# First weight-sum units loaded behind the eighth attention step, summed from the twelfth, and gate columns loaded one step later

## The chip, the cores and the metric

One core of a Trainium2 chip runs the whole program. The metric is the device time of one launch in microseconds (us). Engines: PE does matmuls, DVE elementwise work, ACT activations, POOL small things and the issue of "software" DMAs (queue q0), SP the issue of most other DMAs (queue q1). Times inside a trace are us from the first instruction; the device time is 1.8 us longer than that span. In the lines of a trace, `arena` is the one large on-chip buffer in which the program places most of its tensors, so it stands for many of them.

## The reference

An adaptive-layer-norm transformer block on one prompt of 2048 rows:

```python
h = layernorm(x) * (1 + ca) + sa
q = (h @ wq) -> 32 heads;  k, v: the last 512 cached rows of 4 kv heads
x = x + ga * (softmax(q k^T / sqrt(128)) v) @ wo
h = layernorm(x) * (1 + cb) + sb
x = x + gb * ((silu(h @ w_gate) * (h @ w_up)) @ w_down)
# sa, ca, ga, sb, cb, gb = silu(c) @ w_mod, each 1024 wide
```

## The kernel before

Large products are done as seven smaller ones (Strassen's scheme), for which sums of weight blocks are needed. Each attention runs in 64 numbered steps (0 to 63, then 64 to 127). During the first attention DVE makes those of wo in 16 "units" of 512 KB: POOL loads a unit, DVE makes four sums in two ticks, POOL stores it to DRAM. The second attention does the same for w_down in 14 units.

Every instruction goes through a small tracker. It makes the issuing engine wait for the last writer of what it reads, and for the last writer and *all readers* of what it writes:

```python
def op(self, st, emit, reads=(), writes=()):
    for b in reads:   # wait for b.last_write
    for b in writes:  # wait for b.last_write and for every entry of b.reads
    ...
    for b in reads:   b.reads[st] = c
    for b in writes:  b.last_write = (st, c); b.reads = {}
```

The helpers that the change touches, and the steps of attention that they lie between (cuts marked with `...`):

```python
def unit_load(end):
    ...
    T.op(Q_of[slot][0], lambda: g.dma_start(dst, src), writes=[w.b_raw, w.b_s3])   # g is POOL

def unit_chain(k0, k1):
    unit_load(k1)
    unit_load(k1)
    yield
    for k in range(k0, k1):      # two ticks a unit: two sums; two sums, store, next load
        ...

def pv(i):
    ...                          # 16 matmuls into PSUM banks 5 and 6
    r = i % 2
    T.op(DVE, reciprocal(rl[r] <- PSUM), writes=both + [B_rl[r]])
    T.op(DVE, o_s <- PSUM * rl[r], reads=[B_rl[r]], writes=both + [...])
    ...                          # transposing DMA of o_s

def pre0(i):                     # start of step i of the first attention
    if i in (7, 8):
        load_wga(i - 7)          # 1 MB of gate columns each, needed in steps 12 to 14
    ...
    if i in (8, 9):              # second half of the rows: modulate the transposed norm
        for dt in range(4 * (i - 8), 4 * (i - 8) + 4):
            modulate(hT[1], B_hT[1], dt, ...)
    ...                          # query projection; norm_turn issues the transposes of nsc into hT[1]

# step i: pre0(i); scores(i-1); pv(i-2); tick0(i)
def tick0(i):
    ...
    if i == 8:
        chain[0] = unit_chain(0, HP)
    if 8 <= i < NI - 8:
        unit_tick(i)             # skips i % 4 == 3 and 21..24
```

The softmax here doesn't subtract the row's maximum and nothing guards it: scores larger than these inputs give would overflow.

## Time and profile before

| | before |
|---|---|
| device time, median of the first 3 runs | 1164.04 us (1162.75 to 1164.68) |
| device time of the profiled run, span | 1161.61, 1159.8 us |
| PE busy | 1143.1 us, with 86 of 7105 matmul records missing from this trace |
| wait of the modulation for the transpose | 2.10 us |
| PE idle behind it | 1.97 us |

The missing records are why PE's busy times of different traces are not compared below. What can be compared is the distance between two landmarks: the reciprocal of step 7 and that of step 12. The loads are issued before the first of the two, but every wait of DVE and PE that the change removes or makes in the first attention lies between them. Timeline columns: start, duration, engine, line, operation, and in brackets the idle time just before and what ended it.

```profile
49.99 0.18 DVE L824 RECIPROCAL rl<-ps 128x4 f32<-128x4 f32 x1 [1.19 <-PE ps L272]
...
71.03 0.18 DVE L824 RECIPROCAL rl<-ps 128x4 f32<-128x4 f32 x1 [1.68 <-PE ps L272]
```

The stretch is 71.03 - 49.99 = 21.04 us.

### The profile page before, as it was taken

What the parts mean: (1) busy time and instruction counts of PE and PEld (TensorE: products, weight loads), DVE (VectorE), ACT (ScalarE), POOL (GpSimd) and SP (SyncE); (2) the same over time, 40 slices, a digit from 0 to 9 for tenths busy, and PEclk for the clock granted to TensorE, in tenths of its full rate; (3) what the DMA queues carried; (4) which work ended last, traced back from release to release, by engine and by line L of the source; (5) the groups of instructions that cost most, each with busy time, mean ns of one, the idle gap of its engine ahead of it and who ended that gap; (6) DMA issues with size and microseconds to landing.
All of it is one profiled execution on the core that took longest, in us unless ns stands there. A gap on an engine that the chain in (4) does not pass through costs nothing.

```text
span 1159.8 us, 18164 instructions
## 1 busy us (share of the span) xinstructions
PE 1143.1 (99%) x7019; PEld 588.2 (51%) x7105; DVE 817.5 (70%) x1638; ACT 532.5 (46%) x745; POOL 68.8 (6%) x137
## 2 busy tenths in 40 slices
PE   8899999999999999999999999999999999999999
PEld 5565556654446666556444444444444444444444
DVE  4758997657576777776567898767558777776536
ACT  3866777730117777787110344454110444544110
POOL 1200221000000111111000010000000000000000
PEclk9999999999999999999999999999999999999999
DMA  9878899966906898844865232333764424234443
GB/s 326 178 188 202 217 214 219 204 169 188 261 10 170 190 205 195 212 94 108 202 192 172 78 104 73 102 81 100 209 197 143 123 74 109 73 93 131 131 162 110
DMA packets 289941, 179.98 MB, mean 155 GB/s; under 512 B 130496, under 2 KB 278080, under 8 KB 289856
## 3 DMA queue, kind: packets, MB, share of 16 engines
q1 hardware_dynamic: 226880, 92.31, 35.8%
q10 hardware_dynamic: 54336, 55.05, 14.9%
q0 software_dynamic: 8640, 31.46, 9.1%
q8 instruction: 56, 0.92, 0.3%
q14 instruction: 29, 0.24, 0.1%
HBM read 128.45 MB, written 19.92 MB: 128 GB/s over the span
## 4 chain that ended last, share of the span: by engine, by line
PE 94%; DVE 2%; DMA 1%; ACT 1%; issue 1%; SPq 0%; POOL 0%; DVEq 0%; ACTq 0%
PE ps L272 94%; ACT arena L805 1%; DMA arena<-nsc 1%; DVE arena L835 1%; DMA arena<-in_w_mod_dram 0%; DVE arena L906 0%; PE ps L276 0%; DVE st L413 0%; SPq L310 0%; DVE arena L432 0%; SPq L341 0%; DVE arena L852 0%; ACT tmp L743 0%; DVE arena L1563 0%; ACT L1548 0%
## 5 line engine op out<-in xcount | busy, mean ns | idle before, releaser
L272 PE MATMUL ps<-arena 128*128 128x512 f16 (+2 forms) x6714 | 1135.4, 329 | 13.8 <-POOL arena L406 2.2
L272 PEld LDWEIGHTS ps<-arena 128*128 128x128 bf16 (+1 forms) x6800 | 578.0, 98 | 564.8 <-DVE arena L835 6.3
L805 ACT ACTIVATE arena<-ps 128x1024 bf16<-128x1024 f32 x256 | 261.3, 1021 | 45.9 <-PE ps L272 33.9
L838 ACT ACTIVATE tmp<-ps 128x512 f32<-128x512 f32 x167 | 99.7, 597 | 297.8 <-PE ps L272 283.7
L906 DVE TENSOR_TENSOR arena<-arena 128x512 f16<-128x512 bf16 x328 | 133.5, 420 | 3.0
L835 DVE TENSOR_TENSOR arena<-ps,tmp 128x512 bf16<-128x512 f32 (+1 forms) x134 | 91.9, 686 | 49.3 <-PE ps L272 37.8
L838 ACT ACTIVATE nsc<-ps 128x512 f32<-128x512 f32 x84 | 50.1, 596 | 93.2 <-PE ps L272 90.9
L827 DVE TENSOR_TENSOR arena<-ps,rl 128x512 f16<-128x512 f32 x128 | 88.5, 691 | 4.9 <-DVE rl L824 0.5
L835 DVE TENSOR_TENSOR arena<-ps,nsc 128x512 f16<-128x512 f32 x84 | 57.4, 687 | 41.2 <-PE ps L272 29.9
L824 DVE RECIPROCAL rl<-ps 128x4 f32<-128x4 f32 x128 | 23.1, 180 | 88.0 <-PE ps L272 87.0
L1548 ACT ACTIVATE arena<-arena 128x512 f16<-128x512 f16 x84 | 49.9, 624 | 32.4 <-DVE arena L835 32.4
L1044 DVE TENSOR_TENSOR arena<-arena 128x2048 f16<-128x2048 f16 (+3 forms) x56 | 56.2, 1013 | 9.3 <-PE ps L272 8.8
L1120 DVE TENSOR_TENSOR tmp<-ps,tmp 128x512 f32<-128x512 f32 x32 | 22.1, 690 | 57.0 <-ACT tmp L838 47.3
L838 ACT ACTIVATE arena<-ps 128x512 f32<-128x512 f32 x16 | 9.6, 597 | 89.0 <-PE ps L272 89.0
L956 DVE TENSOR_TENSOR arena<-arena 128x512 f16<-128x512 bf16 x120 | 48.0, 421 | 1.9 <-DMA arena<-in_A_wo_dram 0.8
L413 DVE BATCH_NORM_STATS2 st<-x_res 128x6 f32<-128x512 bf16 x58 | 39.6, 683 | 3.9 <-DMA x_res<-in_A_x_dram 3.7
L1563 DVE TENSOR_TENSOR arena<-arena 128x512 f16<-128x512 f16 x84 | 35.1, 418 | 0.3
L1121 DVE TENSOR_TENSOR tmp<-tmp,rowb 128x512 f32<-128x512 f32 (+1 forms) x49 | 33.6, 686 | 1.7
L427 DVE TENSOR_SCALAR nsc<-x_res,mv,rstd 128x1024 f16<-128x1024 bf16 (+1 forms) x30 | 16.2, 541 | 24.1 <-DMA arena<-nsc 23.4
L603 DVE SCALAR_TENSOR_TENSOR arena<-arena 128x1024 bf16<-128x1024 bf16 x24 | 29.2, 1217 | 0.0
L1122 DVE TENSOR_TENSOR arena<-tmp,x_res 128x512 bf16<-128x512 f32 (+1 forms) x33 | 22.3, 675 | 1.1
L835 DVE TENSOR_TENSOR arena<-ps,rowb 128x512 f16<-128x512 f32 x28 | 19.3, 690 | 3.9 <-ACT rowb L838 3.4
(87 smaller groups left out, 333.9 us busy)
## 6 DMA issues: line engine op xcount, KB each, us to landing
arena<-in_A_wq_dram SPq DMA_DIRECT2D x28, 512.0 KB, 5.2
arena<-wo_sum ACTq DMA_DIRECT2D x7, 2048.0 KB, 8.7
arena<-in_B_w_gate_dram SPq DMA_DIRECT2D x28, 512.0 KB, 4.1
arena<-in_B_w_up_dram SPq DMA_DIRECT2D x28, 512.0 KB, 4.9
arena<-wd_sum ACTq DMA_DIRECT2D x8, 1792.0 KB, 7.8
arena<-in_B_w_down_dram ACTq DMA_DIRECT2D x6, 1792.0 KB, 7.2
arena<-in_A_wo_dram POOLq DMA_DIRECT2D x16, 512.0 KB, 4.9
wo_sum<-arena POOLq DMA_DIRECT2D x16, 512.0 KB, 4.7
```

Source lines behind the costliest of these rows:

```text
L272: T.op(PE, lambda: TE.matmul(out_ap, lhsT, rhs, start=start, stop=stop, skip_group_check=skip), reads=reads, writes=[bank_buf])
L413: T.op(DVE, lambda: V.bn_stats(st_[sl][:, hf * 6:hf * 6 + 6], x_res[:, t, hf * 512:hf * 512 + 512]), reads=[B_x[t]], writes=[B_st[sl]])
L805: T.op(ACT, lambda: A.activation(ex_s[es][:, 2 * kp:2 * kp + 2, :], banks2(SCB + 2 * kp), AF.Exp, scale=att_scale), writes=[PB[SCB + 2 * k ...
L827: T.op(DVE, lambda: V.tensor_tensor(o_s[os_].rearrange("p (a b) d -> p a b d", a=2), psap(PVB * 512, [[512, 2], [130, 2], [1, P]]), rlb, A ...
L835: T.op(DVE, lambda: V.tensor_tensor(out, bank(ba), other, ADD), reads=[ob2], writes=[PB[ba], ob])
L838: T.op(ACT, lambda: A.activation(dst, bank(bk), AF.Copy), writes=[PB[bk], db])
L906: T.op(st, lambda: eng.tensor_tensor(o, a, b, op), reads=rd, writes=[wr])
L956: T.op(DVE, lambda: V.tensor_tensor(o, a, b, SUB), reads=rd, writes=[wr])
L1044: T.op(DVE, lambda: V.tensor_tensor(o, a, b, SUB), reads=rd, writes=[sb])
L1121: T.op(DVE, lambda: V.tensor_tensor(tm, tm, rw, MULT), reads=[B_row[row]], writes=[tb])
L1548: T.op(ACT, lambda: A.activation(o, s_, AF.Silu), reads=[sb], writes=[ob])
L1563: T.op(DVE, lambda: V.tensor_tensor(gu[blk][:, p, :], o, s_, MULT), reads=[sb, ob], writes=[B_gu[blk][p]])
```

## The change

The intent: the two first unit loads, free to start long before their step, crowd the transposing DMAs of the next norm. They are to start later; so are the gate columns; and the sums begin when the data are surely there. To hold the loads back they are declared to read rl, which the attention steps write.

```diff
-            def unit_load(end):
+            def unit_load(end, ahead=()):
...
-                T.op(Q_of[slot][0], lambda: g.dma_start(dst, src), writes=[w.b_raw, w.b_s3])
+                T.op(Q_of[slot][0], lambda: g.dma_start(dst, src), reads=ahead, writes=[w.b_raw, w.b_s3])
...
             def unit_chain(k0, k1):
-                unit_load(k1)
-                unit_load(k1)
+                unit_load(k1, B_rl)
+                unit_load(k1, B_rl)
...
-                if i in (7, 8):
-                    load_wga(i - 7)
+                if i in (8, 9):
+                    load_wga(i - 8)
...
                 if i == 8:
                     chain[0] = unit_chain(0, HP)
-                if 8 <= i < NI - 8:
+                    next(chain[0])
+                if 11 < i < NI - 4:
                     unit_tick(i)
```

## The prediction

> **What bounds the kernel now.** I read the page's busy shares first, then the chain of work that ended last, then the timeline and the waits of the stretch that the change touches.
>
> ```profile
> PE 1143.1 (99%) x7019; PEld 588.2 (51%) x7105; DVE 817.5 (70%) x1638; ACT 532.5 (46%) x745; POOL 68.8 (6%) x137
> PE 94%; DVE 2%; DMA 1%; ACT 1%; issue 1%; SPq 0%; POOL 0%; DVEq 0%; ACTq 0%
> ```
>
> PE is busy 1143.1 of 1159.8 us. The change touches no matmul, so all it can win anywhere is a share of the 16.7 us in which PE stands idle: 1.4% of the span. That alone rules out a gain of 2%. The question is which idle piece goes and what new one comes.
>
> The chain has one large piece that is not PE, between 44.6 and 53.6 us, and the timeline shows both ends of it:
>
> ```profile
> 44.59 8.98 DMA arena<-nsc
> ...
> 43.79 1.69 POOL L945 DMA_DIRECT2D arena<-in_A_wo_dram  x2
> ...
> 49.73 1.00 SPq L580 DMA_DIRECT2D arena<-in_w_mod_dram  x1
> ...
> 53.60 1.38 DVE L432 TENSOR_SCALAR arena<-arena,gain,mod_bf 128x512 f16<-128x512 f16 x4 [2.10 <-DMA arena<-nsc]
> 53.80 0.58 SPq L580 DMA_DIRECT2D arena<-in_w_mod_dram  x1
> 54.90 0.69 DVE L656 CAST arena<-ps 128x512 bf16<-128x512 f32 x1
> 55.49 0.17 DVE L824 RECIPROCAL rl<-ps 128x4 f32<-128x4 f32 x1
> 55.64 6.64 PE L272 MATMUL ps<-arena 128*128 128x512 f16 x38 [1.97 <-DVE arena L656]
> ```
>
> The fourth transposing DMA of the next normed chunk (nsc) was issued at 44.59 us and took 8.98 us; the others of this stretch took 3.1 to 3.3. Only when it had landed could DVE modulate (L432, step 8 of attention); behind that in DVE's order stands the eviction of the query projection (L656), whose PSUM bank PE needs. So PE stood 1.97 us. Why was it slow? Two unit loads of 512 KB had been put on the software queue at 43.79, long before program order of step 8 suggests: they are written in step 8, but POOL has nothing else to do and nothing to wait for. The DMA view of 47 to 50 us shows the collision:
>
> ```profile
> q0 software_dynamic: 246, 0.92, 90.2%
> q1 hardware_dynamic: 259, 0.07, 10.5%
> ```
>
> About as many packets of either queue, but those of the loads carry 4 KB and those of the transposes 256 B: the loads took 90% of the engines' time.
>
> **What the Trainium skill says.** "DMA: Bandwidth & Descriptors", section "Queues, rings and completion order": each DMA engine goes round its queues packet by packet. The trace agrees: 246 packets against 259 in those 3 us, although the bytes stand 13 to 1. Its section "Issuing engines are not separate DMA queues" says that DMAs of all issuing engines run on the same 16 engines and interleave; the same two lines agree. So moving a load in time moves its collision, it doesn't remove its 1 MB. "Trainium Architecture — The Big Picture", section "Inside one NeuronCore": each engine has its own instruction stream and synchronizes only through semaphores; the trace agrees, in that POOL issued step 8's loads at 43.79 while PE was some steps behind.
>
> **The change, part by part.**
>
> (a) The two first loads get the reciprocal buffers rl as a read. POOL now waits for the last reciprocal written before them in the program: that of step 8, which stands at 55.49 above. They leave the stretch 44 to 50. With them the gate columns go from steps 7 and 8 to steps 8 and 9 (49.73 and 53.80 above; one step is about 3.5 us, from the reciprocals at 59.94 and 63.44 below). Then the fourth transpose should take the 3.3 us of its neighbours and land near 48.5. DVE finishes its last older operation (a cast, L626) at 51.5, modulates until 52.9, evicts until 53.5; PE ends its previous work at 53.67. The 1.97 us of PE go. Four short waits of weight loads for the second modulation (1.3 us in the list of waits) stay, since its first part still waits in line behind the reciprocal and the scaling. Gain: 2.0 us.
>
> (b) But the dependence works in both directions. Having read rl, the loads must have landed before DVE may write rl again, in the very next step. DVE works in order, so it stands at step 9's reciprocal:
>
> ```profile
> 59.94 0.18 DVE L824 RECIPROCAL rl<-ps 128x4 f32<-128x4 f32 x1 [1.08 <-PE ps L272]
> ...
> 63.44 0.18 DVE L824 RECIPROCAL rl<-ps 128x4 f32<-128x4 f32 x1 [1.08 <-PE ps L272]
> ```
>
> Moved up by 2.0, step 9's reciprocal is due at 57.95. POOL is released near 53.9 (reciprocal at 53.7). In the trace, from POOL's issue at 43.79 to the first packets is some 1.7 us, so packets flow from about 55.6. They meet the gate columns: 2 MB in 2 KB packets, which the window from 54 to 61 us shows moving at 346 GB/s by themselves (2.42 MB in all). Turn by turn, 4 KB against 2 KB, the loads get two thirds, 230 GB/s: 1.05 MB takes 4.5 us, to 60.1, and with the completion some 60.5 (an estimate). DVE then needs 0.18 + 0.69 us and gaps, so the scaled result frees the PSUM banks at about 61.5. PE meanwhile has the next projection (8 matmuls) and scores (4 matmuls), about 2.6 us of the 3.5 us step, and wants those banks at 57.95 + 2.6 = 60.5. New stall: about 1.0 us, with 0 to 2.5 as limits (a landing from 59.5 to 62).
>
> (c) The same helper starts the second attention's chain, so the same read is put there:
>
> ```profile
> 345.19 1.45 POOL L945 DMA_DIRECT2D arena<-in_B_w_down_dram  x2 [129.78 <-PE ps L272]
> ...
> 349.45 0.18 DVE L824 RECIPROCAL rl<-ps 128x4 f32<-128x4 f32 x1 [2.90 <-PE ps L272]
> ```
>
> The issue there waits for PE anyway, and rl was written long before: no later start. The two landed 4.2 and 4.8 us after issue, so the second at 350.1 to 350.7, and the reciprocal slips 0.7 to 1.2 us. PE's slack before it needs the banks is 2.6 less 0.9 = 1.7 us. Loss: 0.
>
> (d) The sums of the first unit go from steps 9 and 10 to 12 and 13, each later one by one place in the list of ticks, and the last from 53 and 54 to 56 and 57. All steps from 12 to 54 keep the same two operations of about 0.42 us (L956). DVE has room at both ends: 3.79 us busy of 60 to 65, 6.22 of 220 to 230. The sums stored last are first read after the attention, beyond 247 us. Gate columns are needed in step 12, where the matmuls on them begin at 68.46; they should land by 63. Cost: 0.
>
> Sum: -2.0 + 1.0 + 0 + 0 = -1.0 us, from 1164.0 to 1163.0.
>
> **Rivals.** First, the wait for rl eats everything: if POOL's software issue starts late, or the gate columns hold the engines longer than the estimate, landing is at 62 or later; then the new stall is over 2.0 and the time 1164 to 1165. For it: the loads and 2 MB of gate columns are now released within 4 us of each other; against it: PE's 2.6 us of other work. Second, the wait is wholly covered: landing before 59.5, time 1162. For it: undisturbed, the pair landed within 5.5 us of the first issue (53.9 + 5.5 = 59.4); against it: undisturbed is just what they are not. Third, nothing is gained since the transposes were slow for another reason: in 50 to 54 us the DMA engines were held while little moved:
>
> ```profile
> 50.00:54.00 4.00, 3.67 (x32) 2.08 (x29) 1.86 (x5) 3.01 (x4) 0.00 (x0) 1.00 1.51 115
> ```
>
> A share of 1.51 at 115 GB/s is not explained by the loads' bytes, which had mostly passed by 50. If that tail hits the transposes wherever they are, the stall stays and (b) comes on top: 1165. I think it unlikely, since a fourth transpose begun unhindered at 46 is through before this stretch. Fourth, a shifted chain could collide with other loads later, at 14 and 20 steps (x) or with the transposes every fourth step; the pattern by step is the same, so I give it ±0.5 us.
>
> **Range and chances.** The mechanism gives 1161.8 to 1165 around 1163.0; three runs before spread from 1162.75 to 1164.68, about 1 us to each side. So 1160.5 to 1165.8 should hold it 8 times in 10. A 2% gain needs 23.3 us, more than all of PE's idle time; a 2% loss needs some other stall twelve times that of (b), for which I see nothing. Within 2%: 0.98.
>
> **What would show it right or wrong.** In the changed kernel's timeline: POOL's first loads at about 54 us, not 43.8; the nsc transpose landing in 3 to 4 us; no wait of L432 for it and no 1.97 us of PE idle at 53.7; then a wait of the reciprocal of step 9 for the landing of the loads of wo, some 2.5 us on DVE, and about 1 us of PE idle near 60.5. Wrong would be: no such DVE wait (the gain is then the full 2 us), a PE stall of over 2 us there, or the transpose still slow. Step 66's reciprocal near 350 should wait for the loads of w_down without any idle of PE behind it.

## The result, and the profile after

1162.68 us (median of 6 runs, 1161.74 to 1163.10) against 1163.70 for the kernel before (6 runs, 1162.68 to 1165.36): ratio 0.999, with a 95% interval of 0.9977 to 1.0002, so no difference is established. No run of the experiments below reaches 2% either, and what is told apart there are tenths of a per cent. Ratios here and below are the mean time of one kernel's fast runs over that of the other's of the same rounds, so they are not quite the ratio of the medians quoted.

The timeline of the changed kernel, in the stretch that the prediction showed of the one before:

```profile
50.26 0.18 DVE L824 RECIPROCAL rl<-ps 128x4 f32<-128x4 f32 x1 [1.19 <-PE ps L272]
...
51.69 1.37 DVE L432 TENSOR_SCALAR arena<-arena,gain,mod_bf 128x512 f16<-128x512 f16 x4
...
53.98 0.18 DVE L824 RECIPROCAL rl<-ps 128x4 f32<-128x4 f32 x1 [0.33 <-PE ps L272]
...
54.47 1.69 POOL L945 DMA_DIRECT2D arena<-in_A_wo_dram  x2 [10.36 <-DVE rl L824]
...
62.29 0.18 DVE L824 RECIPROCAL rl<-ps 128x4 f32<-128x4 f32 x1 [4.83 <-DMA arena<-in_A_wo_dram]
...
63.34 6.29 PE L272 MATMUL ps<-arena 128*128 128x129 bf16 x52 [2.25 <-DVE arena L827]
...
72.04 0.18 DVE L824 RECIPROCAL rl<-ps 128x4 f32<-128x4 f32 x1 [1.68 <-PE ps L272]
```

The modulation (L432) no longer waits, and step 8's reciprocal comes 3.72 us after step 7's, not 5.50 as before (55.49 - 49.99): 1.78 us won. POOL held the loads until that reciprocal was done. Then step 9's reciprocal stands 4.83 us for them to land, and behind it PE stands 2.25 us, for the scaled result (L827) that frees its PSUM banks. The stretch is 72.04 - 50.26 = 21.78 us: in this pair of profiles it is 0.74 us *longer* than before. Up to step 8's reciprocal 1.78 us are won; from there to step 12's, 2.52 are lost (72.04 - 53.98 = 18.06 against 71.03 - 55.49 = 15.54).

The view of line L454, which issues the transposes, shows what the three nsc transposes issued between 40 and 50 us took to land (minimum, median, maximum), and the queues from 44 to 49 us show one large stream where there were two:

```profile
DMA to landing us min/median/max: 3.1/3.3/3.3
```

```profile
q1 hardware_dynamic: 2762, 0.67, 71.7%
```

No packet of the software queue is left there; the transposes land in 3.3 us, where the last of them took 8.98. The chain of work that ended last now goes through the load instead:

```profile
54.47 0.94 POOL arena L945
55.42 6.75 DMA arena<-in_A_wo_dram
...
63.34 11.85 PE ps L272 x132
```

In the second attention the same back-wait is there, and costs nothing: step 66's reciprocal waits 3.89 us for the loads of w_down, yet PE's line goes on without a break from 342.81 for 15.35 us, in the timeline. POOL's issue is 0.83 us later than before (346.02, not 345.19), the reciprocal 2.10 (351.55, not 349.45), so it slips by about 1.3 us (an estimate from these four times):

```profile
342.81 15.35 PE L272 MATMUL ps<-arena 128*128 128x512 f16 x105
...
346.02 1.45 POOL L945 DMA_DIRECT2D arena<-in_B_w_down_dram  x2 [120.58 <-PE ps L272]
...
351.55 0.18 DVE L824 RECIPROCAL rl<-ps 128x4 f32<-128x4 f32 x1 [3.89 <-DMA arena<-in_B_w_down_dram]
```

### The profile page after: what moved, and what is told of

It reads as the page before. It is cut to its first block, busy times and chain, and to the rows that moved or that the text cites. A ratio compares the mean times of both kernels' runs of the same rounds, so it can differ in the third digit from the quotient of the medians.

```text
span 1160.9 us, 18250 instructions
## 1 busy us (share of the span) xinstructions
PE 1149.0 (99%) x7105; PEld 587.8 (51%) x7105; DVE 816.5 (70%) x1638; ACT 532.5 (46%) x745; POOL 68.7 (6%) x137
## 4 chain that ended last, share of the span: by engine, by line
PE 96%; DVE 2%; ACT 1%; DMA 1%; issue 1%; POOL 0%; DVEq 0%; ACTq 0%; POOLq 0%
PE ps L272 95%; ACT arena L805 1%; DVE arena L835 1%; DMA arena<-in_A_wo_dram 1%; DVE arena L906 0%; PE ps L276 0%; DVE st L413 0%; ACT arena L618 0%; DVE arena L852 0%; DVE arena L850 0%; ACT tmp L743 0%; DVE arena L1564 0%; POOL arena L945 0%; ACT L1549 0%; DVE arena L827 0%
## 5 line engine op out<-in xcount | busy, mean ns | idle before, releaser
L827 DVE TENSOR_TENSOR arena<-ps,rl 128x512 f16<-128x512 f32 x128 | 88.5, 691 | 5.1 <-DVE rl L824 0.8
L956 DVE TENSOR_TENSOR arena<-arena 128x512 f16<-128x512 bf16 x120 | 47.8, 419 | 1.0
```

Of the source, the lines that this page charges most:

```text
L827: T.op(DVE, lambda: V.tensor_tensor(o_s[os_].rearrange("p (a b) d -> p a b d", a=2), psap(PVB * 512, [[512, 2], [130, 2], [1, P]]), rlb, A ...
L956: T.op(DVE, lambda: V.tensor_tensor(o, a, b, SUB), reads=rd, writes=[wr])
```

## The experiments

The theory to test: the loads alone crowd the transpose; holding them back takes that wait away; but the way in which they are held back (a read of rl) puts a new wait on the next step's reciprocal that costs about as much. Rivals: the gate columns were the cause; the relief of DVE in steps 9 and 10 is what acts; the loads' bytes hold PE up wherever they are.

All twelve kernels gave correct results and ran in three groups, each on one chip (the first four, the second four, the last four). A row's "low" counts executions whose mean granted clock was under 1.000; "full clock" is the median of the others. These still spread: one execution of the kernel before took 1165.93 us at 1.000. The stretch is that of the profiled execution.

| run | median us | full clock us | low | stretch us | ratio to before (95%) |
|---|---|---|---|---|---|
| *kernel before, first group* | 1161.83 | 1161.6 | 3 of 11 | | |
| before_again | 1163.33 | 1163.3 | 1 of 6 | 23.40 | 1.0001 (0.9983 to 1.0018) |
| after_again | 1162.76 | 1162.6 | 2 of 6 | 21.10 | 1.0005 (0.9986 to 1.0023) |
| free_order | 1160.12 | 1160.0 | 1 of 6 | 19.26 | 0.9983 (0.9964 to 1.0001) |
| one_rl | 1160.54 | 1160.5 | 1 of 6 | 19.36 | 0.9987 (0.9966 to 1.0007) |
| *kernel before, second group* | 1164.01 | 1163.8 | 6 of 11 | | |
| loads_only | 1165.13 | 1162.6 (one) | 4 of 5 | 24.36 | 1.0004 (0.9990 to 1.0018) |
| gate_only | 1163.06 | 1161.8 | 3 of 6 | 23.29 | 0.9993 (0.9978 to 1.0008) |
| sums_only | 1163.80 | 1161.3 | 3 of 6 | 20.86 | 0.9997 (0.9979 to 1.0015) |
| free_gate_old | 1160.49 | 1160.5 | 0 of 5 | 19.26 | 0.9970 (0.9955 to 0.9984) |
| *kernel before, third group* | 1162.72 | 1162.4 | 3 of 11 | | |
| after_third | 1164.09 | 1162.7 | 3 of 6 | 21.45 | 1.0011 (0.9995 to 1.0028) |
| free_again | 1160.25 | 1160.3 | 0 of 5 | 19.26 | 0.9975 (0.9962 to 0.9988) |
| free_gate_old2 | 1160.07 | 1160.1 | 0 of 5 | 19.27 | 0.9974 (0.9960 to 0.9987) |
| free_sums_old | 1160.91 | 1160.9 | 0 of 5 | 19.50 | 0.9979 (0.9966 to 0.9993) |

The first profiles of before and after have 21.04 and 21.78. The stretch explains the times: device time of the profiled execution less its stretch is 1140.5 to 1141.4 us in thirteen of the fourteen profiles (1161.61 - 21.04 = 1140.57 for the first; the exception is under free_order).

### before_again: the kernel before against itself

No edit.

> Control: the kernel before against itself. Every theory: ratio 1.000 within 0.0015. It shows how far one profile speaks for others: the nsc transpose of step 5 should again take 8 to 9.5 us, DVE's modulation wait about 2 us for it and PE stand about 2 us near 53.7; if that wait varies by more than 1 us between profiles, one pair of profiles cannot carry the sum.

The ratio is 1.0001, but at full clock the two copies differ by 1.7 us, more than the 1.0 between before and after. The profile shows why one pair of profiles can't carry the sum. Timeline, then the windows view (columns: stretch, its length, busy time of PE, PEld, DVE, ACT, POOL, granted clock, DMA share, GB/s):

```profile
55.49 1.38 DVE L432 TENSOR_SCALAR arena<-arena,gain,mod_bf 128x512 f16<-128x512 f16 x4 [3.37 <-DMA arena<-nsc]
...
57.52 14.08 PE L272 MATMUL ps<-arena 128*128 128x512 f16 x92 [3.23 <-DVE arena L656]
```

```profile
55.00:60.00 5.00, 2.48 (x6) 0.87 (x7) 4.05 (x11) 0.13 (x1) 0.00 (x0) 0.76 1.01 322
60.00:65.00 5.00, 5.00 (x34) 2.73 (x33) 2.68 (x6) 2.05 (x2) 0.00 (x0) 0.90 0.50 164
```

The same wait was 3.37 us here, not 2.10, and PE's idle 3.23. Just behind it the granted clock falls, to 0.50 from 58 to 61 us: the two lines stand for 5 x 0.24 + 5 x 0.10 = 1.7 us of lost full speed, so this costs up to 1.7 us (an estimate from these lines). The Trainium skill, "TensorE: Matmul & The Clock Gate", section "Why this matters for your kernels", warns of PE-idle gaps of more than about 3 us, since they bring the clock back to half; this trace agrees, with 3.23 us.

### after_again and after_third: the changed kernel again

No edit.

> Control: the changed kernel again. Theory (the removed wait of 2 us is mostly replaced by a wait of step 9's reciprocal for the landing of the two loads): ratio 0.998 to 1.000, a DVE wait of 4 to 5.5 us for the loads of wo in step 9, PE idle of 1.5 to 2.7 us behind it. Rival (the first profile was a chance one): the DVE wait is under 2.5 us and PE does not stand.

> The changed kernel once more, beside the three that read hT on one chip. Theory: among executions at full clock 1162.3 to 1163.2 us, with the reciprocal of step 9 waiting 4 to 5.5 us for the loads. Rival (its distance from the kernels that read hT was the chip's): under 1161 us at full clock.

The reciprocal of step 9 waited 4.15 and 4.50 us for the loads, and PE stood 1.57 and 1.92 us. The first profile was no chance one. The stretch is 21.10 and 21.45. At full clock the kernel takes 1162.6 and 1162.7 us, which is inside the 1161.6 to 1163.8 of the groups of the kernel before. The ratios, 1.0005 and 1.0011, do not repeat the 0.999 of the first result: whether the change gains or loses is not shown.

### free_order: loads held back by something that is not rewritten

```diff
-            def unit_chain(k0, k1):
-                unit_load(k1, B_rl)
-                unit_load(k1, B_rl)
+            def unit_chain(k0, k1, ahead=()):
+                unit_load(k1, ahead)
+                unit_load(k1, ahead)
...
-                    chain[0] = unit_chain(0, HP)
+                    chain[0] = unit_chain(0, HP, B_hT[1][0:HK])
```

> The loads read the modulated halves of hT, which DVE writes in step 8 and not again for some 25 us, instead of rl; the second attention's chain reads nothing. Theory: the first loads go at about 53 us, the transpose takes 3 to 4 us, no reciprocal waits for a load, PE's 2.25 us of idle in step 10 go: 2 us faster than the changed kernel, 1160 to 1161 us, ratio to before 0.9965 to 0.9985. Rival (the 3 MB of loads hold PE up whatever reads them): as the changed kernel, within 0.5 us.

Faster than the changed kernel by 2.6 us at full clock, as the theory has it, and nothing in step 9 waits for a load. The interval of its ratio, 0.9964 to 1.0001, just takes in 1; free_again below is the firmer run. The profiled execution itself took 1164.10 us for another reason, and is the exception named above. In step 20, behind the stretch, a sum (L956) waited for a later unit load, and PE with it:

```profile
103.48 0.89 DVE L956 TENSOR_TENSOR arena<-arena 128x512 f16<-128x512 bf16 x2 [3.30 <-DMA arena<-in_A_wo_dram]
...
105.24 9.63 PE L272 MATMUL ps<-arena 128*128 128x129 bf16 x72 [2.21 <-DVE arena L827]
```

```profile
105.00:110.00 5.00, 4.76 (x27) 2.99 (x28) 3.67 (x7) 0.36 (x1) 0.71 (x1) 0.66 1.16 348
```

Here the low clock follows at once on 2.21 us of idle. It is the only low-clock execution of the 26 of the kernels that read hT. This is what the prediction's fourth rival feared for step 20, where rows of x are loaded too (issued at 98.95 us); in the other thirteen profiles no sum of the first attention waits over 1.1 us for its load.

### one_rl: only the reciprocal buffer that step 9 doesn't write

```diff
-                unit_load(k1, B_rl)
-                unit_load(k1, B_rl)
+                unit_load(k1, B_rl[0:1])
+                unit_load(k1, B_rl[0:1])
```

> The loads read only rl0, the one written in step 8 (and next in step 10), not rl1, which step 9 writes. Theory: step 9's reciprocal is free; step 10's comes due about 61 us and waits about 1 us for the landing near 62, which is inside PE's slack of 1.7 us: PE idle under 0.5 us, time within 0.5 us of the run that reads hT, 2 us under the changed kernel. Rival (any read of rl costs what the changed kernel loses): as the changed kernel.

Within 0.5 us of free_order, as expected. Step 9's reciprocal is free, and step 10's came 3.90 us after it, in place of the usual 3.50; PE has no idle to show for it:

```profile
58.45 0.18 DVE L824 RECIPROCAL rl<-ps 128x4 f32<-128x4 f32 x1 [1.08 <-PE ps L272]
62.35 0.18 DVE L824 RECIPROCAL rl<-ps 128x4 f32<-128x4 f32 x1 [1.48 <-PE ps L272]
```

The view names PE as the last releaser there, so the wait of 1 us for the landing that was expected is not shown as such. The landing fits all the same: the second load, issued at 55.3, took 6.9 us, to 62.2, just ahead of that reciprocal. What is shown is that the loss comes from the buffer that the very next step rewrites: with one step more of distance it is gone.

### loads_only: the change with the gate columns back in steps 7 and 8

```diff
-                if i in (8, 9):
-                    load_wga(i - 8)
+                if i in (7, 8):
+                    load_wga(i - 7)
```

> The changed kernel with the gate columns back in steps 7 and 8. Theory (the unit loads alone had crowded the transpose): the transpose still takes 3 to 4 us and the 2 us wait of the modulation stays away; the loads, let go near 54.5 us, meet less of the gate columns and land 1 to 2 us sooner, so the reciprocal of step 9 waits 2.5 to 4 us and PE stands 0 to 1.3 us: 1161 to 1162 us, 0.5 to 1.5 below the changed kernel. Rival (the gate columns had slowed the transpose): the modulation waits again 1 to 2 us, time as before or longer.

Half right. The transposes took 3.1 to 3.3 us and the modulation didn't wait, so the gate columns had not slowed them. But the loads landed later, not sooner, and this is the longest stretch of all (behind PE's 3.53 us of idle the clock stood at 0.50 from 64 to 67 us):

```profile
54.23 1.69 POOL L945 DMA_DIRECT2D arena<-in_A_wo_dram  x2 [10.36 <-DVE rl L824]
...
63.32 0.18 DVE L824 RECIPROCAL rl<-ps 128x4 f32<-128x4 f32 x1 [6.11 <-DMA arena<-in_A_wo_dram]
...
64.37 7.60 PE L272 MATMUL ps<-arena 128*128 128x129 bf16 x52 [3.53 <-DVE arena L827]
```

The queues from 54.9 to 57.9 us, after POOL had issued the first load, have but one line with packets:

```profile
q1 hardware_dynamic: 857, 1.05, 108.1%
```

For some 3 us no packet of the software queue moved at all; the gate columns drained first. I had counted on turn by turn. The first packets of the loads came at 58.1 us, 3.9 us after POOL's issue. The changed kernel's trace has the same in small: from 55.0 to 56.5 us only q1 moved packets (290, 0.59 MB), and the loads' first came at 56.9, 2.4 us after issue, as the first half of the gate columns ended; in the kernel before it was 2.1 us (45.9), with the transposes just drained. What the change's shift of the gate columns does is thus shown by comparison: it puts their second half behind the loads, and PE's stall is 1.57 to 2.25 us in three profiles, where it was 3.53 in this one. Why the software queue's packets start so late beside a full q1 (late descriptors, or the engines' choice) is open.

### gate_only: the kernel before with only the gate columns later

```diff
-                if i in (7, 8):
-                    load_wga(i - 7)
+                if i in (8, 9):
+                    load_wga(i - 8)
```

> The kernel before with only the gate columns one step later. Theory: the transpose still takes 8 to 10 us beside the unit loads, the modulation waits 1.5 to 3.5 us and PE stands 1.5 to 3.3: as before, within 0.7 us. Rival (gate columns are the cause): the transpose takes under 6 us and 2 us are gained.

The modulation waited 3.33 us for the transpose, which took 10.27, and PE stood 3.19. The ratio is 0.9993. The median is 0.95 us and the full-clock median 1.9 us under the kernel before of this group, outside the 0.7 that I had given, but two copies of one kernel differed by 1.7, and the stretch of 23.29 us is no shorter. The rival falls by the transpose, which stays slow with the gate columns out of its way:

```profile
55.44 1.38 DVE L432 TENSOR_SCALAR arena<-arena,gain,mod_bf 128x512 f16<-128x512 f16 x4 [3.33 <-DMA arena<-nsc]
```

### sums_only: the kernel before with only the sums later

```diff
-                if 8 <= i < NI - 8:
+                    next(chain[0])
+                if 11 < i < NI - 4:
```

> The kernel before with only the sums moved from the ninth to the twelfth step. Theory: the sums have room wherever they stand: as before, within 0.7 us, same wait of the modulation. Rival (DVE's relief in steps 9 and 10, four operations of 0.42 us, is what gains): 0.8 us or more faster than before.

The transpose took 8.88 us, the wait was 1.93, PE stood 1.79; ratio 0.9997, with a stretch of 20.86 beside 21.04. The full-clock median, of three runs, is 2.4 us lower than that of its group, more than the 0.7 expected; the profile offers no cause for it, and the stretch less PE's stall is that of the kernel before (19.07 against 19.07 us). The interval of the ratio, about 2 us to each side, is too wide to exclude the rival's 0.8 us; the profile speaks against it. I count it as no effect.

### free_gate_old and free_gate_old2: hT read, gate columns not moved

```diff
 # to free_order
-                if i in (8, 9):
-                    load_wga(i - 8)
+                if i in (7, 8):
+                    load_wga(i - 7)
```

> The run that reads hT instead of rl, with the gate columns back in steps 7 and 8. Theory (with no wait on the loads, the place of the gate columns doesn't matter): within 0.5 us of the run that reads hT with the gate columns moved (1160 us on the first chip), about 2 us under the changed kernel; transpose 3 to 4 us. Rival (the gate columns in step 7 reach the transpose): the modulation waits and PE stands over 0.5 us near 54 us, 1161 us or more.

> The kernel that reads hT with the gate columns left in steps 7 and 8, again. Theory: within 0.5 us of the one with the gate columns moved; fewer executions with a granted clock under 1.000 than before and than the changed kernel, since no stall of 2 us or more is left in this stretch. Rival (the low clock comes at random): as many of them as the others.

Ratios 0.9970 and 0.9974, stretches 19.26 and 19.27: with no DVE wait on the loads, the place of the gate columns doesn't matter. The rival that gate columns in step 7 reach the transpose falls here too: the transposes landed in 3.1 to 3.4 us. In the second run no execution of five had a low clock, against 3 of 11 and 3 of 6 of the kernel before and the changed kernel on the same chip; that is as expected, but too few to settle it alone.

### free_again: the kernel that reads hT again

No edit to free_order.

> The kernel that reads hT, gate columns and sums moved as in the change, again. Theory: 1159.8 to 1160.7 us at full clock, 2 to 2.6 under the changed kernel on the same chip, no reciprocal waits for a load in step 9. Rival: within 1 us of the changed kernel.

1160.25 us; ratio 0.9975 with an interval that excludes 1, and 2.4 us under after_third at full clock on the same chip. Its timeline is the plain picture of the theory, without a wait for any load:

```profile
53.31 1.69 POOL L945 DMA_DIRECT2D arena<-in_A_wo_dram  x2 [9.25 <-DVE arena L432]
...
53.93 0.18 DVE L824 RECIPROCAL rl<-ps 128x4 f32<-128x4 f32 x1 [0.32 <-PE ps L272]
...
55.22 11.85 PE L272 MATMUL ps<-arena 128*128 128x512 f16 x86 [0.46 <-DVE arena L432]
...
58.38 0.18 DVE L824 RECIPROCAL rl<-ps 128x4 f32<-128x4 f32 x1 [1.08 <-PE ps L272]
```

Step 8 to step 9 takes 4.45 us, where the changed kernel takes 8.31 (62.29 - 53.98).

### free_sums_old: only the later start, without rl

```diff
 # to free_gate_old
-                if 11 < i < NI - 4:
+                if 9 <= i < NI - 8:
```

> The same with the sums back in the ninth step, so that of the change only the later start of the loads is left, without rl. Theory (whatever DVE operation stands in line behind the loads takes over the wait): the loads land near 62 us, the first sum waits some 2 to 4 us for them in step 9 behind the scaling of its own step, and holds up the projection's eviction: PE stands 1 to 3 us there, 1161 to 1163 us. Rival (the sums need not move once rl is free): within 0.5 us of the run above.

Mostly a miss. The first sum needs only the first of the two loads, which took 7.0 us from 53.33 and had landed by 60.4 us, so it waited little:

```profile
60.39 0.88 DVE L956 TENSOR_TENSOR arena<-arena 128x512 f16<-128x512 bf16 x2 [1.08 <-DMA arena<-in_A_wo_dram]
```

The stretch grows by 0.24 us, and the full-clock median by 0.8 us beside free_gate_old2. The 0.8 us are over the rival's 0.5 and under the theory's 1 us of stall. The wait does pass on to the next DVE operation that needs the loads, but it is small; moving the sums is worth some tenths.

## Why the prediction was right or wrong

The time was right: 1163.0 was predicted, 1162.68 measured, and "within 2%" holds. The mechanism was right as well, in both its parts, but two terms of the sum were mis-sized, and that the number is so close is partly luck. The net -1.0 us is not established (ratios 0.999, 1.0005 and 1.0011), and in the pair of profiles the stretch grew by 0.74. The sum took its stall of 1.97 us from an execution of 1161.61 us and its base from the median, 1164.04. From the profiled execution the way is 1161.61 - 1.78 + 2.52, plus 0.4 outside the stretch, = 1162.7. The base was 2.4 us too high for that stall and the net 2.1 too low, so the two errors nearly cancel.

- **(a) Loads and gate columns later: -2.0 us.** Right in kind. The transposes land in 3.3 us, and loads_only and gate_only show that it is the loads and not the gate columns. In the profile shown, the reciprocals give -1.78. But the size of what is removed varies from execution to execution: in the four profiles with early loads PE stood 1.97, 3.23, 3.19 and 1.79 us, and after the two long ones the clock fell as well. I took one profile's stall for the stall. The third rival, that the transposes were slow for another reason, falls: they landed in 3.1 to 3.4 us in all ten profiles in which the loads are held back. Against the 19.26 of the kernels without either wait, the four have 1.6 to 4.1 us too much.
- **(b) The new wait for the landing: +1.0 us.** Right in place, too small in size: PE stood 2.25, 1.57 and 1.92 us, mean 1.9. The step that failed is the landing "60.5 (an estimate)", and in it the turns with the gate columns. It was 62.2. Of the 1.7 us, 0.6 is the later release (54.47, not 53.9) and 0.7 the later start of the packets, 2.4 us after issue and not 1.7; the remaining 0.4 is the end of the transfer. The sharing at two thirds of the rate was not seen: the loads' packets came only as the first half of the gate columns ended, and then moved 0.99 of their 1.05 MB from 56.9 to 60.5 us, 275 GB/s, beside 0.20 MB on q1. The last packets passed after 60.5, beside the second half of the gate columns. In loads_only, with both halves in front, the loads waited 3.9 us for their first packet. The first rival of the prediction, "landing is at 62 or later" with a stall over 2.0, is what the first profile shows; its time of 1164 to 1165 did not follow. That (a) was larger in most timed runs would explain it, but those runs have no trace: what is shown is that the two profiled executions with a stall of 3.2 us took 1164.6 us, and those with under 2 us 1161.6 and 1161.3.
- **Readings of the trace that were off.** The 1.7 us from POOL's issue to the first packets are 2.1 in that trace (43.79 to 45.9). The pair that "landed within 5.5 us of the first issue" took 5.4 and 6.4 us, each from its own issue, and the issues lie 0.9 us apart: at least 6.3 from the first. A 2% loss would need over twenty times the stall of (b), not twelve.
- **(c) The second attention: 0.** Right: the reciprocal slips, and PE goes on without idle. Its wait of 3.89 us is not a delay of that size: the slip was about 1.3 us, of the 0.7 to 1.2 predicted, since before the reciprocal had waited 2.90 us for PE.
- **(d) Shifted sums, late gate columns: 0.** Right by sums_only and gate_only, within what two copies of one kernel differ by. That the sums have to wait for loads that start later is shown by free_sums_old, at some tenths of a us.
- **The range.** The kernel before had a spread that I read as noise. Part of it is the varying stall and the clock behind it. Low-clock executions: 12 of 33 of the kernel before in the three groups, 5 of 12 of the changed kernel there (0 of 6 in the first result), 1 of 26 of the five that read hT. No term of the prediction stood for it.

So the gain of the change went into a wait that the change itself made: a read of rl delays the loads, and as a reader's mark it also delays the next writer of rl until the loads have landed. With hT as the buffer read, the modulated half is written in step 8 too and not again until step 23 (L852, at 108.9 us in free_again), long after the landing, and the same delay is had without the wait: 1160.1 to 1160.5 us, ratios 0.9970 to 0.9983 to the kernel before, of which all but free_order's exclude 1. That version beats the kernel before by 0.2 to 0.3%, and the changed kernel by 2.4 to 2.6 us at full clock on the same chip (no interval was computed for that pair). What stays open: why the same kernel's transposes land at 8.9 us in one execution and at 10.3 in another, and what delays the software queue's packets beside a full q1.

## What to carry to other kernels

To hold a transfer back, tie it to a value that is ready at the right time and that nobody rewrites soon: in a tracker that knows readers, every "wait for this" is also a "don't overwrite this until I have landed". Look for the wait that such a tie puts on the next writer: when is that write due, and will the transfer have landed by then? And when a stall of 2 us or more on PE varies between executions, profile it more than once, and look at the granted clock just behind it.

## What the Trainium skill lacked or had wrong

- "DMA: Bandwidth & Descriptors", "Queues, rings and completion order": turns packet by packet were seen where transposes and loads were both under way (246 packets against 259), but the loads' first packets came only as the gate columns on q1 ended: in loads_only none moved from 54.9 to 57.9 us while q1 moved 857, although POOL had issued at 54.23; the first came 3.9 us after issue, against 2.4 in the changed kernel and 2.1 in the kernel before. The page doesn't say when a software load's packets begin beside a busy hardware queue.
- "TensorE: Matmul & The Clock Gate", "Why this matters for your kernels": gaps of more than about 3 us are named; in one execution, of free_order, the clock fell behind a gap of 2.21 us, while gaps of 2.25 and 1.97 us in other executions did not bring it down. So a gap under 3 us was once enough here.
- No page says that the time of a DMA transpose of 256 KB beside a 1 MB load on the software queue goes from 3.3 us to 8.9 or 10.3 in these runs.
